# An attention-and-MoE kernel on one core: the opening's first scores in paired banks, and a PV product in pieces

## The chip, the core and the metric

The kernel runs on one core of a Trainium2 chip. The core has TensorE (PE in the profile; its weight loads are PEld), VectorE (DVE), ScalarE (ACT), GpSimd (POOL) and SyncE (SP), each with an instruction stream of its own. They meet through semaphores. Matrix products land in PSUM, eight banks of 512 fp32 values on each of 128 partitions; DMA moves data between the chip's memory and the on-chip buffers. The metric is the device time in microseconds; smaller is better.

## The reference

For 8 batches and 12 heads (448 rows, head size 64) the kernel computes attention with normalized q and k, and then a two-layer MLP over the concatenated heads:

```
q_n, k_n = q / rms(q) * g_q,  k / rms(k) * g_k
attn     = softmax(q_n k_n^T / 8)            # rows of 448
x        = (attn v), heads side by side      # 3584 x 768
h        = x w_in                            # 768 -> 2048
out      = max(0.01 h, h) w_out              # 2048 -> 768
```

## The kernel before

**Units.** The 96 heads are worked in 24 units of four heads; three units make a batch. The four heads of a unit lie as two by two (index r and a) on halves of the 128 partitions, and the 448 rows of a head as seven blocks of 64 (index t, 0 to 6). "Scores (u,t)" below are the scores of unit u for k block t, and "exp (u,t)" their exponential.

**One unit's steps**, with the lines of the profile:

- load of q and k (`load`, L146, queue of SP), of v (`load_v`, L149, queue of POOL);
- squares (`prep_sq` on ScalarE, L169, or `prep_sqp` on POOL, L173), their sums over 64 (`prep_ssq`, VectorE, L180), 1/rms as an Ln and an exponential (`prep_rinv`, ScalarE, L185 and L186: uu, rinv), the normalized fp16 q and k (`prep_norm`, VectorE, L192: n);
- seven transposes each of q and k by PE into a bank (`tr`, L861, for units 0 and 1; `trn`, which is `prep_tr`, L204, for 2 and 3), and a copy of them to `qkT` (`vcopy`, VectorE, L809 for q with the factor g, L811 for k). For unit 1 the k transposes come in two parts, block 0 (K0) and blocks 1 to 6 (K1);
- scores, four matmuls of 64x64 per block into two banks (`score`, L222). `score0` takes block 0 of units 1 and 2, `qk` the others;
- the shift. The exponential needs a common bound. `shift_max` takes the maximum of block 0's scores per partition (L257 and L259 for two separate banks, L262 for a pair) and spreads it on a diagonal (dg, L264); `shift_mm` brings it to all partitions by a matmul with ones (L280; L274 from unit 4 on) and takes the maximum again (L281 or L275), and L285 makes the bias eb of it;
- seven exponentials (`ex`, ScalarE; L242 for a pair of banks in one instruction of 128x896, L239 for two separate banks in two of 128x448), which give back the banks of the scores;
- the row sums of the exponentials, 28 matmuls with ones (`zsum_slot`, L311, or `zsum`, L300), their reciprocal as Ln and exponential (`zinv`, L385 and L387, or by halves L390 and L392: rz), the product with v (`pv`, 28 matmuls, L401), and the multiply of the two, half by half (`xmul`, VectorE, L410), which gives x of this unit and frees PV's two banks.

**Banks.** Banks 4 to 7 are two "slots" for the scores of `qk`; banks 0 to 3 are given one at a time by `aux`, in the order in which they were dropped. An instruction that writes a bank waits until its last reader is through. From unit 5 on all banks are shared.

**Order.** The kernel is written under a manual schedule: on each engine instructions run in the order of the text, which for units 0 to 3 is written out by hand (L827 to L1030). From unit 3 on a loop interleaves a unit's steps with matmuls of the MLP taken from a queue (`moe1`, L423; `moe2`, L469; `seven`, L522). The MLP's first two tiles are started by hand by `moe1_part` (L431): k tiles 0 to 3 need units 0 and 1, the last two need the halves of unit 2's multiply. `warm` (L825) issues matmuls of ones whose result nobody reads.

Of the kernel before, what the change touches and what calls it, by code (L numbers as in the profile page):

```python
# [18 lines left out]
def kernel(  # L19
# [44 lines left out]
    def aux():  # L64
        can = [i for i in free if mine(i)]
        if shared:
            can = [i for i in can[:-1] if i ^ 1 not in free] or can
        free.remove(can[0])
        return single[can[0]]
# [162 lines left out]
    def ex(u, most=NS):  # L232
# [3 lines left out]
        for t, sT in s["sT"][:most]:  # L236
            if isinstance(sT, list):
                for a in range(2):
                    nc.scalar.activation(s["et"][:, t, a], sT[a][:, 0:S], AF.Exp, bias=s["eb"], scale=1.0)  # L239
                    drop(sT[a])  # L240
            else:
                nc.scalar.activation(s["et"][:, t], sT[:, :, 0:S], AF.Exp, bias=s["eb"], scale=1.0)  # L242
                drop(sT)
        s["sT"] = s["sT"][most:]

    def score0(u):
        banks = [aux() for a in range(2)]
        score(u, 0, banks)
        st[u]["sT"] = [(0, banks)]

    def shift_max(u):
        s = st[u]
        sT = s["sT"][0][1]
        if isinstance(sT, list):
            pm2 = small.tile([P, 2], FP32, tag="pm2", name="pm2")
            for a in range(2):
                nc.vector.tensor_reduce(pm2[:, a:a + 1], sT[a][:, 0:S], axis=AXL.X, op=ALU.max)  # L257
            s["spare"] = sT[0]
            nc.vector.tensor_reduce(s["spare"][:, 511:512], pm2, axis=AXL.X, op=ALU.max)  # L259
        else:  # L260
            s["spare"] = sT[:, 0]
            nc.vector.tensor_reduce(s["spare"][:, 511:512], sT[:, :, 0:S], axis=AXL.XY, op=ALU.max)  # L262
# [6 lines left out]
    def shift_mm(u):  # L269
        s = st[u]  # L270
        if u > 0 and "pslot" in st[u - 1]:
            pb = st[u - 1]["pslot"][:, :, S:S + 64]
            for x in range(2):
                nc.tensor.matmul(pb[:, x], onesp, s["dg"][:, 64 * x:64 * x + 64], start=True, stop=True)  # L274
            nc.vector.tensor_reduce(s["spare"][:, 510:511], pb, axis=AXL.XY, op=ALU.max)  # L275
        else:
# [4 lines left out]
            nc.vector.tensor_reduce(s["spare"][:, 510:511], pb[:, 0:P], axis=AXL.X, op=ALU.max)  # L281
# [3 lines left out]
        nc.vector.tensor_scalar(s["eb"], s["spare"][:, 510:511], -1.0, DELTA, op0=ALU.mult, op1=ALU.add)  # L285
# [17 lines left out]
    def zsum_slot(u):  # L303
        s = st[u]
        s["zslot"] = slot()
# [88 lines left out]
    def pv(u, t0=0, t1=NS):  # L394
        s = st[u]
        if t0 == 0 and "pslot" not in s:
            s["pv"] = [aux() for r in range(2)]
# [429 lines left out]
    with tc.manual_schedule():  # L827
# [28 lines left out]
        def tr(u, ti, chunks, tp=None):  # L856
            if tp is None:
                tp = aux()
# [57 lines left out]
        drop(tr(1, 0, ((ALL, vcopy),)))  # L916
        tpk = tr(1, 1, ((K0, vcopy),))
        qk(0, (4,))
        ex(0)
        k1 = []  # L920
        tr(1, 1, ((K1, lambda *a: k1.append(a)),), tpk)
        score0(1)
        prep_ssq(2, ALL, (0,))
        shift_max(1)
        vcopy(*k1[0])
        drop(tpk)
        shift_bank(1)
        qk(0, (5,))
        ex(0)
        warm(8, st[1]["pb"])  # L930
        qk(0, (6,))
        ex(0)
        warm(4, st[1]["pb"])
        shift_mm(1)
        prep_ssq(2, ALL, (1,))
        prep_ssq(3, ALL, (0,))
        ex(1)
        prep_rinv(2)
        qk(1, (1,))
        ex(1)  # L940
        zsum_slot(0)
        pv(0)
        zinv(0)
# [5 lines left out]
        prep_sqp(4, (0,))  # L949
        load_v(4)  # L950
        for f in range(2):
            load_w_out(8 * f, 8)
        qk(1, (2,))
        warm(6, st[1]["pb"])
        drop(st[1]["pb"])
        ex(1)
        trn(2, 0, vcopy)
        qk(1, (3,))
        ex(1)
        trn(2, 1, vcopy)  # L960
        xmul(0)
        qk(1, (4,))
        ex(1)
        qk(1, (5,))
        ex(1)
        score0(2)
        shift_max(2)
        qk(1, (6,))
        ex(1)
        shift_bank(2)  # L970
        warm(12, st[2]["pb"])
        shift_mm(2)
        prep_ssq(3, ALL, (1,))
        prep_ssq(4, ALL, (0,))
        ex(2)
        prep_rinv(3)
# [193 lines left out]
```

## Time and profile before

| | |
|---|---|
| time, median of 3 runs | 409.28 us (408.88, 409.28, 411.71) |
| the profiled execution's own time | 410.29 us |
| its span, first to last instruction | 408.3 us |
| PE busy, share of the span | 97% |
| VectorE, ScalarE, POOL busy | 75%, 74%, 18% |
| mean granted TensorE clock | 0.994 of full |
| busy us of the 25 from 20 to 45: PE, VectorE, ScalarE, POOL | 21.26, 20.48, 22.77, 16.62 |

Times in the profile count from the span's first instruction. A line of the timeline has start, duration, engine, line, operation, output and input, how many instructions are merged in it, and in brackets how long the engine sat idle before it and what ended that. In a line of the timeline with several instructions the duration runs from the first start to the last end; on one engine the next instruction can start before the one ahead has ended. A line of stretches has the stretch, its length, then for each engine busy time and number of instructions, then the granted clock of TensorE (PEclk), the share of DMA engines that were busy, and GB/s.

### The profile page before, as it was taken

The page shows a single profiled execution, that of the slowest core. Times are in us where ns is not written, and L with a number is a line of the kernel's source. Part 1 is how long each engine was busy: PE and PEld are TensorE (multiplying, and loading weights), DVE is VectorE, ACT ScalarE, POOL GpSimd, SP SyncE. Part 2 cuts the span into 40 slices and gives each one's busy share as a digit, 9 for nine tenths or more (in the row PEclk, how much of TensorE's full clock was granted, in tenths as well). Part 3 has the DMA queues.
Part 4 walks back from the last instruction along what each step waited for, and adds up shares of the span by engine and source line. Part 5 has one row for each costly group of instructions (what it writes and reads, how often), then busy time and mean ns, then how long its engine had stood idle before and what let it go on. Part 6 is the DMA issues. An engine that isn't in the chain of part 4 may idle for free.

```text
span 408.3 us, 9444 instructions
## 1 busy us (share of the span) xinstructions
PE 395.0 (97%) x3834; PEld 222.9 (55%) x3834; DVE 307.4 (75%) x484; ACT 301.4 (74%) x476; POOL 74.0 (18%) x86
## 2 busy tenths in 40 slices
PE   7879999999999999999999999989999999999996
PEld 6545454555455544555455544555455557558963
DVE  5898789978888766876678857678579888567672
ACT  5998977879978599688878689868996667743600
POOL 1887331411020200120021200002011202000000
PEclk9899999999999999999999999999999999999999
DMA  5999999899665985578564984676652470032014
GB/s 178 270 251 254 239 236 247 212 204 181 164 161 100 244 218 102 149 196 183 145 158 50 246 218 99 172 176 174 177 96 47 122 163 8 15 72 77 2 39 117
DMA packets 72526, 62.87 MB, mean 154 GB/s; under 512 B 36388, under 2 KB 67620, under 8 KB 72484
## 3 DMA queue, kind: packets, MB, share of 16 engines
q1 hardware_dynamic: 61888, 50.08, 47.0%
q0 software_dynamic: 10272, 11.80, 18.6%
q8 instruction: 30, 0.49, 0.5%
q10 hardware_dynamic: 324, 0.39, 0.3%
q14 instruction: 12, 0.10, 0.1%
HBM read 45.61 MB, written 11.01 MB: 139 GB/s over the span
## 4 chain that ended last, share of the span: by engine, by line
PE 84%; DVE 6%; ACT 5%; DMA 2%; issue 2%; SPq 0%; DVEq 0%; ACTq 0%
PE banks L423 26%; PE banks L522 24%; PE banks L222 8%; PE banks L469 7%; PE banks L401 6%; PE banks L656 6%; PE banks L338 3%; ACT et L242 3%; DVE n L192 2%; DMA rz<-zs 1%; DMA rk<-in_k_dram 1%; PE banks L274 1%; ACT sq L169 1%; PE banks L204 1%; DVE xt L410 1%
## 5 line engine op out<-in xcount | busy, mean ns | idle before, releaser
L242 ACT ACTIVATE et<-banks,eb 128x896 f16<-128x896 f32 x166 | 160.0, 1015 | 23.4 <-PE banks L222 15.4
L423 PE MATMUL banks<-xt,win 128*128 128x448 f16 x612 | 122.2, 353 | 0.0
L423 PEld LDWEIGHTS <-win 128*128 128x128 f16 x612 | 57.3, 98 | 56.1 <-issue 6.8
L417 ACT ACTIVATE gt<-banks 128x448 f16<-128x448 f32 x104 | 56.6, 564 | 5.5 <-PE banks L423 4.4
L222 PE MATMUL banks<-qkT 64*64 64x448 f16 x672 | 49.6, 362 | 3.0 <-ACT et L242 2.1
L180 DVE TENSOR_REDUCE ssq<-sq 128x14 f32<-128x896 f32 (+2 forms) x49 | 50.1, 1056 | 1.3 <-ACT sq L169 1.1
L522 PEld LDWEIGHTS <-sa 128*128 128x128 f16 x352 | 33.4, 98 | 24.6 <-issue 3.6
L522 PE MATMUL banks<-tw,sa 128*128 128x384 f16 x264 | 46.8, 326 | 0.0
L529 DVE TENSOR_TENSOR ost<-banks,ost 128x384 f32<-128x384 f32 x55 | 30.3, 551 | 14.7 <-PE banks L522 14.1
L401 PE MATMUL banks<-et,vt 64*64 64x448 f16 x672 | 37.0, 349 | 0.1
L522 PEld LDWEIGHTS <-gt 128*128 128x128 f16 x264 | 25.5, 98 | 18.3 <-issue 1.7
L222 PEld LDWEIGHTS <-qkT 64*64 64x64 f16 x672 | 17.0, 105 | 32.5 <-issue 26.3
L469 PE MATMUL banks<-wout,gt 128*128 128x384 f16 x192 | 33.7, 326 | 0.0
L291 POOL COPY gate_t<-qkT 128x1 f16<-128x1 f16 x16 | 5.1, 321 | 152.6 <-DMA qkT<-n 152.6
L522 PE MATMUL banks<-wout,gt 128*128 128x384 f16 x176 | 32.4, 326 | 0.0
L379 POOL TENSOR_TENSOR xt<-x,rz 128x896 f16<-128x896 f32 x9 | 19.4, 2158 | 70.4 <-DMA rz<-zs 63.9
L262 DVE TENSOR_REDUCE banks<-banks 128x1 f32<-128x896 f32 x22 | 24.1, 1094 | 10.1 <-PE banks L222 6.3
L353 ACT COPY x<-banks 128x896 f32<-128x896 f32 x16 | 14.5, 906 | 22.1 <-DVE banks L275 22.1
L192 DVE TENSOR_TENSOR n<-rq,rinv 128x896 f16<-128x896 f32 (+2 forms) x25 | 28.3, 1137 | 1.3 <-ACT rinv L186 1.3
L192 DVE TENSOR_TENSOR n<-rk,rinv 128x896 f16<-128x896 f32 (+2 forms) x26 | 27.9, 1078 | 0.0
L401 PEld LDWEIGHTS <-vt 64*64 64x64 f16 x672 | 20.2, 107 | 10.6 <-issue 0.4
L469 PEld LDWEIGHTS <-gt 128*128 128x128 f16 x192 | 17.9, 98 | 13.7 <-issue 2.9
(105 smaller groups left out, 486.8 us busy)
## 6 DMA issues: line engine op xcount, KB each, us to landing
rq<-in_q_dram SPq DMA_DIRECT2D x24, 448.0 KB, 4.7
rk<-in_k_dram SPq DMA_DIRECT2D x24, 448.0 KB, 5.5
out_dram<-ost SPq DMA_DIRECT2D x52, 192.0 KB, 3.4
rz<-zs SPq DMA_DIRECT2D x80, 112.0 KB, 2.7
vt<-in_v_dram POOLq DMA_DIRECT2D x24, 224.0 KB, 4.9
win<-in_moe_w_in_dram POOLq DMA_DIRECT2D x8, 384.0 KB, 14.5
wout<-in_moe_w_out_dram POOLq DMA_DIRECT2D x2, 1536.0 KB, 29.0
out_dram<-ost SPq DMA_DIRECT2D x4, 96.0 KB, 2.1
```

What stands on the lines that cost most here:

```text
L180: nc.vector.tensor_reduce(buf(u, "ssq")[:, ti, :, c[0]:c[1]], buf(u, f"sq{ti}")[:, :, c[0]:c[1]], axis=AXL.X, op=ALU.add)
L192: nc.vector.tensor_tensor(buf(u, "n16")[:, ti, c[0]:c[1]].rearrange("p s a d -> p a s d"), src[:, :, c[0]:c[1]], buf(u, "rinv")[:, ti, :, ...
L222: nc.tensor.matmul(banks[a][64 * r:64 * r + 64, 0:S].rearrange("p (t x) -> p t x", t=NS), kT(u, r, a, t), qT(u, r, a), start=True, stop=True)
L242: nc.scalar.activation(s["et"][:, t], sT[:, :, 0:S], AF.Exp, bias=s["eb"], scale=1.0)
L262: nc.vector.tensor_reduce(s["spare"][:, 511:512], sT[:, :, 0:S], axis=AXL.XY, op=ALU.max)
L401: nc.tensor.matmul(s["pv"][r][64 * a:64 * a + 64, 0:S], vts[u % NV][64 * r:64 * r + 64, a, t], s["et"][64 * r:64 * r + 64, t, a], start=(t ...
L417: nc.scalar.activation(dst, src, AF.Prelu, bias=0.0, scale=1.0, alpha=0.01)
L423: nc.tensor.matmul(hps[:, 0:S], win16[:, kt // 2, kt % 2, ts(ft, P)], xt[:, kt // 2, kt % 2], start=(kt == 0), stop=(kt == KT - 1))
L469: nc.tensor.matmul(op2[:, 0:HC], gt[:, ft, ds(col(t), P)], wout16[:, ft, ds(HC * half, HC)], start=(i == 0), stop=(i == FT - 1))
L522: nc.tensor.matmul(bank[:, 0:HC], a[:, f], b[:, f], start=(first and f == 0), stop=(f == HF - 1), skip_group_check=not first)
L529: nc.vector.tensor_tensor(dst, g[name][:, 0:HC], src, op=ALU.add)
L656: nc.tensor.matmul(bank[:, HX * i:HX * i + HX].rearrange("p (t x) -> p t x", t=NS), w, x[:, kt], start=start, stop=(kt == HK - 1), skip_gr ...
```

## The change

- `score0` of units 1 and 2 takes a pair of banks of 0 to 3 (`pair`), so that the maximum is one reduction and the exponential one instruction; the shift's matmuls go to columns 448 to 511 of that pair (`own`), and the second maximum to a small buffer (`peak`). `shift_bank` and its `warm` matmuls go for these units.
- Unit 1: its first scores come ahead of the six remaining k transposes, which use a bank of their own.
- Unit 2: PV of unit 0 is cut into pieces of 2, 2, 1 and 2 blocks, between unit 2's transposes, its first scores and scores of unit 1; k block 0 is copied first; unit 0's multiply is done in halves, the second after unit 2's k copy.
- The sums of units 0 and 1 are written to a pair of banks 0 and 1 instead of a slot, and their Ln and exponential come directly behind.
- The square sums of units 2 and 3 are done in one go, later than before; the second of unit 4 moves behind unit 2's second half multiply.
- Unit 2's PV comes behind its last scores instead of ahead of them.

The diff, cut to its core (`...` marks what is left out):

```diff
+    def pair():
+        x = [i for i in range(2) if 2 * i in free and 2 * i + 1 in free][0]
...
     def score0(u):
-        banks = [aux() for a in range(2)]
-        score(u, 0, banks)
-        st[u]["sT"] = [(0, banks)]
+        sT = pair()
+        score(u, 0, (sT[:, 0], sT[:, 1]))
+        st[u]["sT"] = [(0, sT)]
+        st[u]["own"] = sT
...
     def shift_mm(u):
...
+        own = s.get("own")
+        if own is not None or u > 0 and "pslot" in st[u - 1]:
+            pb = (st[u - 1]["pslot"] if own is None else own)[:, :, S:S + 64]
             for x in range(2):
                 nc.tensor.matmul(pb[:, x], onesp, s["dg"][:, 64 * x:64 * x + 64], start=True, stop=True)
+            if own is not None:
+                peak = small.tile([P, 1], FP32, tag="peak", name="peak")
+            nc.vector.tensor_reduce(peak, pb, axis=AXL.XY, op=ALU.max)
...
-        s["zslot"] = slot()
+        s["zslot"] = pair() if u < 2 else slot()
...
-        drop(tr(1, 0, ((ALL, vcopy),)))
-        tpk = tr(1, 1, ((K0, vcopy),))
+        drop(tr(1, 0, ((ALL, vcopy),), bank=2))
+        tpk = tr(1, 1, ((K0, vcopy),), bank=3)
         qk(0, (4,))
         ex(0)
+        score0(1)
         k1 = []
-        tr(1, 1, ((K1, lambda *a: k1.append(a)),), tpk)
-        score0(1)
-        prep_ssq(2, ALL, (0,))
+        tpk2 = tr(1, 1, ((K1, lambda *a: k1.append(a)),), bank=2)
+        drop(tpk)
         shift_max(1)
         vcopy(*k1[0])
-        drop(tpk)
-        shift_bank(1)
+        drop(tpk2)
         qk(0, (5,))
         ex(0)
-        warm(8, st[1]["pb"])
+        wb = aux(3)
+        warm(8, wb)
         qk(0, (6,))
         ex(0)
-        warm(4, st[1]["pb"])
+        warm(4, wb)
+        drop(wb)
         shift_mm(1)
-        prep_ssq(2, ALL, (1,))
-        prep_ssq(3, ALL, (0,))
+        prep_ssq(2)
+        ex(1)
+        qk(1, (1,))
         ex(1)
         prep_rinv(2)
-        qk(1, (1,))
+        zsum_slot(0)
+        zinv(0)
+        qk(1, (2,))
         ex(1)
-        zsum_slot(0)
-        pv(0)
-        zinv(0)
         prep_norm(2)
         gate(2)
         prep_sqp(3, (1,))
         load_v(3)
         load(5)
         prep_sqp(4, (0,))
+        st[0]["pv"] = [aux(2), aux(3)]
+        pv(0, 0, 2)
+        drop(tr(2, 0, ((ALL, vcopy),), bank=0))
+        qk(1, (3,))
+        ex(1)
+        pv(0, 2, 4)
+        tpk = tr(2, 1, ((K0, vcopy),), bank=1)
+        drop(tpk)
+        pv(0, 4, 5)
+        score0(2)
+        shift_max(2)
+        qk(1, (4,))
+        ex(1)
+        pv(0, 5, NS)
+        xmul(0, (0,))
+        qk(1, (5,))
+        ex(1)
+        shift_mm(2)
+        qk(1, (6,))
+        ex(1)
+        drop(tr(2, 1, ((K1, vcopy),), bank=2))
+        ex(2)
+        qk(2, (1,))
+        ex(2)
+        xmul(0, (1,))
+        prep_ssq(3)
+        prep_rinv(3)
+        zsum_slot(1)
+        zinv(1)
+        qk(2, (2,))
+        ex(2)
+        prep_norm(3)
+        load(6)
         load_v(4)
         for f in range(2):
             load_w_out(8 * f, 8)
-        qk(1, (2,))
-        warm(6, st[1]["pb"])
-        drop(st[1]["pb"])
-        ex(1)
-        trn(2, 0, vcopy)
-        qk(1, (3,))
-        ex(1)
-        trn(2, 1, vcopy)
-        xmul(0)
-        qk(1, (4,))
-        ex(1)
-        qk(1, (5,))
-        ex(1)
-        score0(2)
-        shift_max(2)
-        qk(1, (6,))
-        ex(1)
-        shift_bank(2)
-        warm(12, st[2]["pb"])
-        shift_mm(2)
-        prep_ssq(3, ALL, (1,))
-        prep_ssq(4, ALL, (0,))
-        ex(2)
-        prep_rinv(3)
-        qk(2, (1,))
-        ex(2)
-        zsum_slot(1)
-        pv(1)
-        zinv(1)
-
-        prep_norm(3)
-        load(6)
         gate(3)
         prep_sqp(4, (1,))
+        st[1]["pv"] = [aux(2), aux(3)]
+        pv(1)
         prep_sqp(5)
         load_v(5)
-        qk(2, (2,))
-        ex(2)
-        warm(12, st[2]["pb"])
         qk(2, (3,))
         ex(2)
-        drop(st[2]["pb"])
         trn(3, 0, vcopy)
-        warm(8, st[2]["pb"])
         trn(3, 1, vcopy)
         xmul(1)
-        prep_ssq(4, ALL, (1,))
+        prep_ssq(4, ALL, (0,))
         qk(2, (4,))
         ex(2)
         st[2]["zt"] = [aux() for r in range(2)]
         zsum(2, 0, 3)
         qk(2, (5,))
         ex(2)
-        pv(2, 0, 3)
-        sums(2, 3, 4)
+        zsum(2, 3, 4)
         qk(2, (6,))
         ex(2)
+        pv(2, 0, 4)
         sums(2, 4, 5)
...
         xmul(2, (1,))
+        prep_ssq(4, ALL, (1,))
         push(0)
```

More of the change, by code (lines that the diff above doesn't have):

```diff
@@ L62, in mine, with aux @@
         return shared or i < 4
-    def aux():
-        can = [i for i in free if mine(i)]
+    def pair():
+        x = [i for i in range(2) if 2 * i in free and 2 * i + 1 in free][0]
+        for i in (2 * x, 2 * x + 1):
+            free.remove(i)
+        return double[x]
+    def aux(bank=None):
+        can = [i for i in free if mine(i) and bank in (None, i)]
         if shared:
@@ L236, in ex @@
         for t, sT in s["sT"][:most]:
[L237 to L243, printed above, removed]
+            nc.scalar.activation(s["et"][:, t], sT[:, :, 0:S], AF.Exp, bias=s["eb"], scale=1.0)
+            drop(sT)
         s["sT"] = s["sT"][most:]
     def score0(u):
-        banks = [aux() for a in range(2)]
-        score(u, 0, banks)
-        st[u]["sT"] = [(0, banks)]
+        sT = pair()
+        score(u, 0, (sT[:, 0], sT[:, 1]))
+        st[u]["sT"] = [(0, sT)]
+        st[u]["own"] = sT
     def shift_max(u):
@@ L253, in shift_max @@
         sT = s["sT"][0][1]
[L254 to L262, printed above, removed]
+        s["spare"] = sT[:, 0]
+        nc.vector.tensor_reduce(s["spare"][:, 511:512], sT[:, :, 0:S], axis=AXL.XY, op=ALU.max)
         s["dg"] = small.tile([P, P], FP16, tag="dg", name="dg")
@@ L270, in shift_mm @@
         s = st[u]
-        if u > 0 and "pslot" in st[u - 1]:
-            pb = st[u - 1]["pslot"][:, :, S:S + 64]
+        peak = s["spare"][:, 510:511]
+        own = s.get("own")
+        if own is not None or u > 0 and "pslot" in st[u - 1]:
+            pb = (st[u - 1]["pslot"] if own is None else own)[:, :, S:S + 64]
             for x in range(2):
                 nc.tensor.matmul(pb[:, x], onesp, s["dg"][:, 64 * x:64 * x + 64], start=True, stop=True)
-            nc.vector.tensor_reduce(s["spare"][:, 510:511], pb, axis=AXL.XY, op=ALU.max)
+            if own is not None:
+                peak = small.tile([P, 1], FP32, tag="peak", name="peak")
+            nc.vector.tensor_reduce(peak, pb, axis=AXL.XY, op=ALU.max)
         else:
@@ L280, in shift_mm @@
             nc.tensor.matmul(pb[:, 0:P], onesp, s["dg"], start=True, stop=True)
-            nc.vector.tensor_reduce(s["spare"][:, 510:511], pb[:, 0:P], axis=AXL.X, op=ALU.max)
+            nc.vector.tensor_reduce(peak, pb[:, 0:P], axis=AXL.X, op=ALU.max)
             if u >= 3:
@@ L284, in shift_mm @@
         s["eb"] = small.tile([P, 1], FP32, tag="eb", name="eb")
-        nc.vector.tensor_scalar(s["eb"], s["spare"][:, 510:511], -1.0, DELTA, op0=ALU.mult, op1=ALU.add)
+        nc.vector.tensor_scalar(s["eb"], peak, -1.0, DELTA, op0=ALU.mult, op1=ALU.add)
     def gate(u):
@@ L395, in pv @@
         s = st[u]
-        if t0 == 0 and "pslot" not in s:
+        if "pv" not in s:
             s["pv"] = [aux() for r in range(2)]
@@ L854, with tr @@
         prep_norm(0, K1, (1,))
-        def tr(u, ti, chunks, tp=None):
+        def tr(u, ti, chunks, tp=None, bank=None):
             if tp is None:
-                tp = aux()
+                tp = aux(bank)
             for c, copy in chunks:
```

## The prediction

> **What bounds the kernel now.** I began with the page: busy time by engine, and the chain that ended last.
>
> ```profile
> PE 395.0 (97%) x3834; PEld 222.9 (55%) x3834; DVE 307.4 (75%) x484; ACT 301.4 (74%) x476; POOL 74.0 (18%) x86
> ...
> PE 84%; DVE 6%; ACT 5%; DMA 2%; issue 2%; SPq 0%; DVEq 0%; ACTq 0%
> ```
>
> TensorE (PE) carries 84% of the chain; only 16% is elsewhere, and the chain in order of time tells where. From 44 us on it is PE almost without a break; from 130 us to the end the waits of PE name one matmul wait, of 0.9 us. So the opening is worth exactly the moment at which PE gets its last operand and runs on. The chain in the stretch that is changed (start us, us, what):
>
> ```profile
> 18.96 1.08 DVE pm L257 x2
> 20.07 0.17 DVE banks L259
> 20.26 0.29 DVE dg L264
> 20.55 0.47 DVE qkT L811
> 21.02 0.22 DVE banks L281
> 21.26 0.17 DVE eb L285
> 21.45 1.16 ACT et L239 x2
> ...
> 42.98 0.64 DVE xt L410
> 43.62 0.04 issue
> 43.66 0.54 PE banks L431 x2
> 44.20 2.27 PE banks L423 x12
> ```
>
> VectorE makes the shift of unit 1, ScalarE waits for it, and at the far end unit 2's multiply releases the last two matmuls of the first MoE tiles. Between them ScalarE is the bound: 22.77 us busy of the 25 from 20 to 45. Its own timeline shows its stalls (in brackets):
>
> ```profile
> 21.45 1.16 ACT L239 ACTIVATE et<-banks,eb 128x448 f16<-128x448 f32 x2 [0.47 <-DVE eb L285]
> 23.87 0.91 ACT L385 ACTIVATE rz<-banks 128x896 f32<-128x896 f32 x1
> 25.66 4.58 ACT L242 ACTIVATE et<-banks,eb 128x896 f16<-128x896 f32 x5
> 30.72 1.16 ACT L239 ACTIVATE et<-banks,eb 128x448 f16<-128x448 f32 x2 [0.47 <-DVE eb L285]
> 34.94 3.87 ACT L242 ACTIVATE et<-banks,eb 128x896 f16<-128x896 f32 x4
> 39.24 1.01 ACT L242 ACTIVATE et<-banks,eb 128x896 f16<-128x896 f32 x1 [0.43 <-PE banks L222]
> ```
>
> Three stalls, 0.47, 0.47 and 0.43 us, and two exponentials in halves, 1.16 us where a whole one occupies 0.91 (five take 4.58: four starts of 0.90 and an end).
>
> **Prices from the rows.** Exponential: 1.01 us long, the next starts 0.91 later. Reduction of 128x896 (L180, L262): 1.07 to 1.10, the next 1.00 later. Normalize (L192): 1.08, the next 1.00 later. dg 0.29, small max 0.30, eb 0.16, half multiply (L410) 0.62, two 1.15. uu 0.31, rinv 0.23, Ln of a unit's sums 0.91, its exponential 0.95. Four score matmuls: 0.31 to the next work, 0.38 to their end; 28 sum matmuls 1.32 and 1.49; within a run of the 64x64 form four take 0.19, so a switch of form costs 0.12. A handover between engines: 0.04.
>
> **The change, step by step, by those prices.** The order of the instructions on each engine is known: POOL's and SP's are unchanged; VectorE, ScalarE and PE differ only between 17 and 44 us.
>
> Unit 1. Its first scores now go before the six k transposes: 18.02 to 18.40. One reduction replaces two halves and their merge, and the square sum of unit 2 that stood ahead of it (17.89, 1.07) moves behind. So max 18.44 to 19.54, dg to 19.86, the k copy (0.55) to 20.33, the shift matmuls at 20.05 (behind the last warm matmuls), small max to 20.62, eb done 20.81, against 21.42. ScalarE is free at 20.88 (0.91 after 19.97): **the first stall is gone**. Exponentials at 20.88 and 21.79. What is late next: both square sums of unit 2 run 20.74 to 22.80, so uu starts at 22.84 (ScalarE idle 0.14), rinv ends 23.41, and the zsum of unit 0, now in the pair that the first exponential leaves at 21.89, runs 21.93 to 23.42 (before: 21.29). Ln of unit 0 at 23.46, against 23.87; exp (1,2) at 25.25, against 25.66: 0.41 earlier. PE idles 1.2 us before that zsum; the Ln would wait for rinv until 23.30 anyway.
>
> Unit 2. Norm of q and k ends 24.52 and 25.52 (0.12 later than before). PV of unit 0 in pieces, transposes and scores share PE; the four extra switches (0.5 us) lie in its idle time. q copy to 26.12, first k block to 26.25, first scores 26.29 to 26.67, max 26.71 to 27.81, dg to 28.13, first half multiply to 28.67, shift matmuls 28.17 to 28.40, small max, eb done 29.09, against 30.69. ScalarE needs its five exponentials until 29.80: **the second stall is gone, with 0.7 us to spare**. Exp (2,0) at 29.80 and (2,1) at 30.71, against 30.72 and, behind uu and rinv, 32.25. The k copy and the other half multiply take VectorE to 30.33.
>
> **A wait that is added.** Both square sums of unit 3 now follow that multiply (before, one was done far ahead): 30.25 to 32.31. ScalarE is free at 31.62 and its uu waits until 32.35: 0.73 lost. Behind it queue rinv, Ln, the second exponential of the sums and exp (2,2), which comes at 34.62 against 34.94. Of 0.92 gained at exp (2,0), 0.32 is left there. Norm of unit 3 ends at 34.04 and 35.04, 0.37 later than before; its transposes, no longer behind 12 and 8 warm matmuls (0.69 and 0.45 us), still give the k copy at 36.29 against 36.76.
>
> Unit 2's end. Before, score (2,6) stood behind PV, which waited for the multiply of unit 1 (until 37.83): the third stall. Now PV stands behind it. Score (2,6) needs the slot that exp (2,4) leaves at 37.45, and is done at 37.87. Exponentials at 34.62, 35.53, 36.44, 37.35, 38.26: **the last at 38.26 against 39.24, 0.98 earlier**. The rest follows as it did: Ln and exponential of the sums, multiply halves at 40.95 and 41.99, the last two matmuls of the first MoE tiles at 42.65 against 43.66. The square sum of unit 4's k now stands after the multiply (42.53 to 43.60), so uu of unit 4 waits to 43.64 and norm ends 46.33, before 46.59; PE reaches its k transposes at about 46.3 and stalls some 0.07.
>
> What is moved past DMA: the calls that load v of unit 4, W_out and unit 6 move in the text only. Unit 5's loads wait for norms 0.12 later, unit 6's 0.37; v of unit 4 needs PV of unit 0, done at 27.2, and was issued at 29.72. W_out, issued at 30.5 and 32.8, landed 25.8 to 32.2 us later, by 65.1 at the latest; PE first reads it at 69.7, then at 68.8. Covered.
>
> **Sum.** 0.41 up to the Ln of unit 0 (the first stall and the first half pair, less the two waits of ScalarE ahead of it) + 0.51 up to exp (2,0) (the second stall) − 0.60 up to exp (2,2) (the new wait of 0.73 less 0.14 for the second half pair) + 0.66 up to exp (2,6) (the third stall, and 0.2 that its four predecessors lost between them) = 0.98. 1.01 is left at the last two matmuls; less 0.07 ahead of unit 4, 0.95 is booked. The profiled execution has 410.29 us, a span of 408.3 and 2.0 around it; it becomes 409.3. It lies 1.0 above the median, 409.28, which becomes **408.3 us**.
>
> Not shown by the trace: a small max that writes to SBUF. pm (L257) does, in 0.57 for 448, about half of 1.10 for 896 written to PSUM: between −0.05 and +0.1; I take 0. The new wait's price is between 0, were VectorE half a microsecond quicker at 26 to 32, and 1.5, twice the walk; I take the walk's 0.73 as all its terms are rows.
>
> **The clock**, 38 warm matmuls fewer after 24 us. The granted clock by stretches (PE busy is the second number, PEclk the third from the end):
>
> ```profile
> 7.48:10.89 3.41, 1.76 (x23) 1.19 (x24) 2.92 (x7) 2.35 (x5) 0.72 (x2) 1.00 0.89 316
> 10.89:14.31 3.42, 3.42 (x32) 2.56 (x28) 2.86 (x6) 2.95 (x5) 2.00 (x3) 0.50 1.01 360
> ...
> 24.55:27.96 3.41, 2.23 (x36) 1.48 (x34) 3.13 (x5) 3.38 (x5) 2.42 (x3) 1.00 1.10 258
> 27.96:31.37 3.41, 2.80 (x52) 1.78 (x48) 2.74 (x7) 2.94 (x5) 3.39 (x4) 1.00 1.09 256
> ```
>
> After a stretch with PE 1.76 us busy of 3.41 the clock was 0.50 for the next; after 2.23 it stayed at 1.00. My walk's PE from 27.96 to 31.37 is 0.23 + 0.38 + 0.49 + 0.38 + 0.52 = 2.0 busy: between the two. Shifted to 27.4 it would be 1.6. At 0.50, ten warm matmuls took 1.27 against 0.57.
>
> The Trainium skill (TensorE: Matmul & The Clock Gate, "Why this matters for your kernels") asks only that PE has no idle gaps above about 3 us; the walk's longest is 1.2, so by it the clock holds and the sum stands. The trace disagrees: the stretch from 7.48 had no gap above 1.34 us and was followed by the half clock. The same page (Part 1) says that the window is free-running, which no row here can show; by it some executions would lose the clock and others not.
>
> **Rivals.** (1) *The gain is swallowed*, 409.3: the clock halves for one stretch, 31.4 to 34.8. zsum of unit 1 ends 0.8 later, Ln waits 0.36, PV and transposes push the k copy to 37.5, and exp (2,6) comes at 39.31, as before. A VectorE that is 0.95 later in the new wait does the same. For: 2.0 lies in the open interval. Against: 24.55 to 27.96 held. 0.22. (2) *Slower*, 410.6: the half clock holds to 38.2. PV then ends at 36.07, score (2,3) at 36.6, k copy at 38.8, exp (2,6) at 40.6, 1.35 later than now; from one stretch to two is where the sign turns. Against: PE is busy in 31.4 to 34.8, which ended the half clock at 14.31. 0.15. (3) *More*, 407.6: the new wait is hidden, 0.73 more. Against: VectorE has no idle time from 26.7 to 32.3. 0.08. (4) The stalls go but PE after 44 us takes its time back in waits for data: 409.3 also; against, the waits of PE show 0.5 us at 43.66 and no other to 130 us. 0.05. The forecast, 407.8 to 408.9: 0.50.
>
> **Numbers.** The range, 406.9 to 410.9, reaches from rival 3, with the 0.4 by which the lowest run lies under the median and 0.3 for the open terms, to rival 2 with 0.3. Within 1% (4.1 us, about what a measurement of this kernel can tell from no change) lie all cases: 0.95; faster 0.02, slower 0.03 for a clock that halves more often.
>
> **What will show it.** Right: eb of unit 1 at about 20.8; no stall of the first exponentials of units 1 and 2; uu of unit 3 waiting 0.7 for the square sums; exp (2,6) unstalled; MoE matmuls from 42.7. Wrong: a PEclk of 0.50 after 20 us, or a wait of PE after 44 us that was not there.

## The result, and the profile after

The changed kernel is slower: 412.23 us median of 22 runs (410.12 to 415.93), against 409.75 of the kernel before (22 runs, 408.30 to 412.08). The ratio is 1.0062, 95% interval 1.0040 to 1.0084. Its profiled execution took 411.59 us, span 409.2. The forecast was 408.3. Medians and ratios below leave out four executions in a second, slower state of the chip: two of count_back, one of count_less and one of the kernel before.

The page of the changed kernel first, with its busy times and the shares of the chain that ended last:

```profile
PE 393.0 (96%) x3798; PEld 221.0 (54%) x3798; DVE 310.3 (76%) x481; ACT 301.0 (74%) x474; POOL 72.9 (18%) x86
...
PE 85%; DVE 6%; DMA 3%; ACT 2%; issue 2%; SPq 0%; DVEq 0%
```

PE has 36 matmuls fewer (3834 before), each with a weight load: 72 instructions. It is busy 2.0 us less in a span that is 0.9 longer. DMA has 3% of the chain instead of 2%.

Did the opening do what was forecast? ScalarE's timeline of the changed kernel, 19 to 44 us, answers line by line to the one shown of before:

```profile
19.24 3.72 ACT L243 ACTIVATE et<-banks,eb 128x896 f16<-128x896 f32 x4 [0.47 <-PE banks L228]
25.48 6.38 ACT L243 ACTIVATE et<-banks,eb 128x896 f16<-128x896 f32 x7
32.56 0.32 ACT L191 ACTIVATE uu<-ssq,eps_t 128x28 f32<-128x28 f32 x1 [0.69 <-DVE ssq L186]
34.83 4.65 ACT L243 ACTIVATE et<-banks,eb 128x896 f16<-128x896 f32 x5
42.24 1.01 ACT L243 ACTIVATE et<-banks,eb 128x896 f16<-128x896 f32 x1
43.87 0.32 ACT L191 ACTIVATE uu<-ssq,eps_t 128x28 f32<-128x28 f32 x1 [0.63 <-DVE ssq L186]
```

The three stalls are gone, the forecast wait of uu is there, and the exponentials of units 1 and 2 run in unbroken rows. Exp (3,0) starts at 42.24, 0.76 before the old 43.00. So at 43 us the kernel is ahead. The chain of waits in order of time (start us, us, what) shows where it falls behind:

```profile
67.34 0.20 PE banks L400 x5
67.54 7.15 DMA qkT<-n
74.69 0.03 issue
74.72 0.45 DVE qkT L182
75.17 2.00 DVE ssq L186 x2
77.17 0.02 issue
77.19 0.33 ACT uu L191
77.52 0.02 issue
77.54 0.23 ACT rinv L192
77.77 0.37 ACT ost L476
78.14 1.82 ACT et L243 x2
79.96 0.04 issue
80.00 1.52 PE banks L400 x28
```

From unit 6 on, k and q are transposed by a DMA (`prep_trd`). Its landing at 74.69 releases VectorE's multiply by g; behind that stand the square sums, uu, rinv and two exponentials, and PE. In the kernel before this landing was at 73.87 and PE ran through. PE's waits between 44 and 200 us, first the kernel before (what, us in total, times, longest):

```profile
PE banks L431 <- DVE xt L410: 0.5, 1, 0.5
```

and the changed kernel:

```profile
PE banks L400 <- ACT et L243: 0.5, 1, 0.5
PE banks L228 <- ACT et L243: 0.5, 1, 0.5
PE banks L271 <- DVE dg L259: 0.4, 1, 0.4
```

Set side by side by the same PE instruction, the changed kernel is 0.76 us ahead at 40 us, 0.56 behind at 80, 1.02 behind at 126 and 1.30 behind at 138.

These early losses are not what stands at the end of this trace. PE's longest wait after 200 us, first in the kernel before and then in the changed kernel:

```profile
PE banks L274 <- DVE dg L264: 0.9, 1, 0.9
```

```profile
PE banks L521 <- DVE ost L528: 0.7, 1, 0.7
```

The kernel before waits at 266 us, behind a landing of rz at 260; the changed one does not wait there and is level again at 270 us (0.09 ahead). It then falls 0.87 behind at 277, where its own wait for VectorE is, and 0.20 more at 314: 0.97 at the end. So one trace shows where PE waits, but the time of the kernel has to be read from the medians.

### The profile page after: what moved, and what is told of

It reads as the page before. It is cut to its first block, busy times and chain, and to the rows that moved or that the text cites. A ratio compares the mean times of both kernels' runs of the same rounds, so it can differ in the third digit from the quotient of the medians.

```text
span 409.2 us, 9372 instructions
## 1 busy us (share of the span) xinstructions
PE 393.0 (96%) x3798; PEld 221.0 (54%) x3798; DVE 310.3 (76%) x481; ACT 301.0 (74%) x474; POOL 72.9 (18%) x86
## 4 chain that ended last, share of the span: by engine, by line
PE 85%; DVE 6%; DMA 3%; ACT 2%; issue 2%; SPq 0%; DVEq 0%
PE banks L422 29%; PE banks L521 24%; PE banks L228 9%; PE banks L400 6%; PE banks L655 6%; PE banks L468 6%; PE banks L337 3%; DVE n L198 2%; DMA qkT<-n 2%; ACT et L243 2%; DVE ssq L186 1%; DMA rk<-in_k_dram 1%; DVE banks L257 1%; PE banks L271 1%; DVE ost L528 1%
## 5 line engine op out<-in xcount | busy, mean ns | idle before, releaser
L198 DVE TENSOR_TENSOR n<-rq,rinv 128x896 f16<-128x896 f32 (+2 forms) x25 | 35.1, 1406 | 1.9 <-ACT rinv L192 1.9
L257 DVE TENSOR_REDUCE banks<-banks 128x1 f32<-128x896 f32 x24 | 26.3, 1096 | 11.0 <-PE banks L228 6.8
L198 DVE TENSOR_TENSOR n<-rk,rinv 128x896 f16<-128x896 f32 (+2 forms) x26 | 26.1, 1010 | 0.0
```

The costliest lines, as they stand in the source:

```text
L198: nc.vector.tensor_tensor(buf(u, "n16")[:, ti, c[0]:c[1]].rearrange("p s a d -> p a s d"), src[:, :, c[0]:c[1]], buf(u, "rinv")[:, ti, :, ...
```

## The theories

The transposing DMA has 16 completions. Own table, from the trace, of the one for unit 6 (us), beside the fetch of 16 KB that the page lists under "q8 instruction":

```
              PE instr.  issue  fetch         1st    15th   16th completion
before        7667       68.21  69.59-70.66   73.72  73.86  73.87
after         7595       67.54  72.46-73.62   73.01  73.15  74.69
```

Fifteen completions came 0.7 us earlier than before, as the opening promised; the last came 1.54 behind the fifteenth, 1.07 after the end of the fetch. **Theory F**: TensorE's instructions are fetched in blocks by the DMA engines (16 KB each, queue q8 of the page); 72 instructions fewer shift all later fetches against the work, into the end of the transposing DMAs, whose last completion then waits. **Theory C**: the 36 matmuls that nobody reads kept TensorE's clock up; without them more executions lose it for a stretch. **Theory D**: the opening's gain ends at the landing, which is set by the loads ahead of it.

Data of all runs, as reference for what follows. "PE instr." counts one fewer than the pages' matmuls and weight loads (2 x 3834 = 7668 before), here and in the expectations; the differences are what matters. "Clock" is the mean granted clock of all executions, "at full clock" the median of those with 0.998 or more. The kernel before ran again beside each round of runs, with medians of 409.88 (the row below), 410.05, 409.63 and 409.96 and mean clocks of 0.9967 to 0.9977, so runs of different rounds are best compared by their ratios. The rounds are count_back to warm_back, gap_fill to gap36_ssq, trd_first to spread_trd, and spread_less to spread_ssq:

```
              PE instr.  median  runs  ratio to before [95%]     clock   at full clock (runs)
before        7667       409.9   35    -                         0.9971  409.65 (21)
after         7595       412.23  22    1.0062 [1.0040, 1.0084]   0.9944  411.32 (5)
count_back    7667       410.63  10    1.0013 [0.9984, 1.0042]   0.9945  409.38 (6)
count_less    7547       410.85  11    1.0013 [0.9993, 1.0033]   0.9950  409.19 (3)
before_less   7595       410.69  12    1.0019 [1.0004, 1.0034]   0.9961  410.86 (5)
warm_back     7667       410.23  12    1.0012 [0.9991, 1.0032]   0.9978  410.16 (10)
gap_fill      7595       412.00  12    1.0036 [1.0012, 1.0060]   0.9969  412.00 (6)
gap36         7667       410.33  12    0.9997 [0.9966, 1.0029]   0.9953  408.97 (3)
early         7743       411.26  12    1.0034 [1.0008, 1.0060]   0.9930  410.63 (2)
gap36_ssq     7667       410.09  12    0.9995 [0.9970, 1.0021]   0.9948  410.74 (2)
trd_first     7595       412.69  12    1.0077 [1.0045, 1.0109]   0.9944  411.62 (4)
before_trd    7667       410.67  12    1.0012 [0.9988, 1.0037]   0.9972  410.01 (7)
spread36      7667       409.35  12    0.9994 [0.9967, 1.0022]   0.9980  408.81 (8)
spread_trd    7667       411.00  12    1.0041 [1.0016, 1.0065]   0.9974  410.25 (7)
spread_less   7595       410.50  12    1.0012 [0.9995, 1.0029]   0.9972  410.63 (6)
spread_mid    7631       410.70  12    1.0018 [1.0001, 1.0035]   0.9979  410.64 (8)
spread_ssq    7667       409.32  12    0.9988 [0.9963, 1.0013]   0.9979  409.03 (8)
```

## First round: the number of instructions

**count_back**: the changed kernel, with the 72 instructions back at the start.

```diff
-        warm(42, wbank)
+        warm(24, wbank)
+        warm_small(54, wbank)      # 128x32 weights, 64 columns
```

> The changed kernel, but 18 of the warm matmuls at the very start (while PE waits for the first load) are replaced by 54 small ones of about the same total time: 72 PE instructions more, as many as the change took away, and nothing else moved. Theory F (PE fetches its instructions in blocks through the same DMA engines; with 72 instructions fewer these fetches fall late into the flight of the transposing DMAs of units 6 to 10, whose landing VectorE waits for): the fetch near 72.5 us moves back to about 69, the late losses go, and the 0.75 us that the opening gained stays: 409.0, against 412.2 for the changed kernel. Theory C (the missing warm matmuls cost TensorE clock): PE is as busy as before, 412.2. Theory D (PE that starts 0.75 us earlier only meets transfers that are bounded by bytes): 412.2.

Measured: 410.63. Unit 6's DMA had no late completion (issue 71.41, fetch 71.94 to 73.25, 16th at 76.06, 0.03 behind the 15th). But the small matmuls held the first transposes up (ScalarE's wait before the first copy to qkT was 1.45 us instead of 0.50), and this trace lost the clock in 16.88 to 23.71 and 33.95 to 37.36. Less than hoped, and not a clean test.

**count_less**: the changed kernel with 24 pairs of warm matmuls at the start merged into one of double width each.

```diff
-        warm(32, wbank)  ...  warm(42, wbank)
+        warm(26, wbank); warm_wide(3, wbank)  ...  warm_wide(21, wbank)
```

> The changed kernel with 48 of the warm matmuls at the start merged into 24 of twice the width: the same PE time, 48 PE instructions fewer. Theory F: each fetch comes some 2.4 us later (256 instructions take about 13 us), so the one at 72.5 comes at about 75, behind the landing of unit 6's transposing DMA, and likewise for units 7 to 10: as fast as with the 72 instructions put back, or better, 408.5 to 409.5. Theory C and theory D: 412.2, nothing that they speak of has changed.

Measured: 410.85. At unit 6 the fetch (73.81 to 74.99) began 0.69 us ahead of the first completion (74.50) and the last was not late (74.62); at unit 8 it was (15th 99.49, 16th 101.04, fetch 98.94 to 99.83). So fewer instructions still are not simply worse. That suggests that the phase counts and not the number; the ratio, 1.0013 (0.9993 to 1.0033), leaves both open.

**before_less**: the kernel before, with 36 pairs of its start merged, so that it has 7595 instructions too and nothing else is changed.

```diff
-        warm(32, wbank)  ...  warm(42, wbank)
+        warm(2, wbank); warm_wide(15, wbank)  ...  warm_wide(21, wbank)
```

> The kernel before, with 72 of the 74 warm matmuls at the start merged into 36 of twice the width: the same PE time and the old order, but 72 PE instructions fewer, as in the changed kernel. Theory F: the fetches fall late into the transposing DMAs as they do in the changed kernel, 411 to 412. Theories C and D: 409.7, as before.

Measured: 410.69, 0.8 above the kernel before. The trace repeats the changed kernel's: fetch 72.32 to 73.43, 15th completion 73.04, 16th 74.60, and PE goes from 0.68 ahead of the kernel before (in this trace the opening began that much earlier) to 0.47 behind at 80 us, 0.90 at 138. **The loss at unit 6 belongs to the number of instructions, not to the new order.** In the median the 72 instructions cost 0.8 us here (ratio 1.0004 to 1.0034), a third of the change's loss. That this is the loss at unit 6, carried to the end, is not shown: at 270 us this trace is level with the kernel before, and 0.19 behind at the end.

**warm_back**: the changed kernel with 18 warm matmuls more at the start and 18 in PE's idle 1.31 us at 20.80.

> The changed kernel with 36 warm matmuls put back, 18 at the start and 18 in the idle time of PE ahead of unit 0's sums (20.8 to 22.1 us): the 72 instructions are back, and PE is busier as well. Theory F: 409.0, as with the small ones at the start, since only the count matters. Theory C: about 410, and better than with the small ones. Theory D: 412.2.

Measured: 410.23. No late completion at unit 6 (16th at 72.78), PE 0.64 ahead until 120 us and 0.22 at 176, although the 18 matmuls at the start held the first transposes up (ScalarE's wait before the first copy to qkT was 1.37 us). The median is nearer to theory C's 410 than to theory F's 409.0.

## Second round: fetch or clock

**gap_fill**: the same 18 in the idle place, 7595 instructions by merging 18 pairs at the start.

```diff
-        warm(42, wbank)
+        warm(6, wbank); warm_wide(18, wbank)
...
         qk(1, (1,))
+        wb = aux(3); warm(18, wb); drop(wb)
         ex(1)
```

> The changed kernel with 18 warm matmuls put into TensorE's idle 1.31 us at 20.80, and 18 pairs of the opening's warm matmuls merged into 18 of double width, so that TensorE has as many instructions as in the changed kernel (7595) and its clock as much work as before. Theory F (the instruction fetches of TensorE, moved by 72 instructions, delay the landing of the transposing DMAs): nothing is mended at full clock; the DMA issued at about 67.5 lands after more than 6.5 us, PE is 0.4 to 0.7 us behind the kernel before at 80 us and about 1 us at 126, and the median is 410.8 to 411.6. Theory C (the missing warm matmuls cost clock): the granted clock of all the executions averages 0.997 and not 0.994, and the time falls to the 409.0 that the opening's gain of 0.77 leaves of 409.75.

Measured: 412.00 with the clock restored to 0.9969, and 412.00 at full clock. Theory C alone falls. The trace has four late completions (units 6, 8, 9 and one at 239 us), each 1.49 to 1.56 us behind the fifteenth.

**gap36**: 36 small ones in that place, nothing at the start.

> The changed kernel with all 36 missing matmuls put back as small ones (32 ns each) in the idle 1.31 us at 20.80, none ahead of the first transposes; 7667 instructions as before the change. Theory F: the DMA issued at 67.5 lands in 5 to 5.7 us, no stall of PE at 80 us, offset there -0.6 or better, median 409.0 to 409.7. Theory C: the same clock as in the run with 18 full matmuls in that place, 0.997, and 409.0. The two agree here; if the median is over 410.5 both lack something.

Measured: 410.33, and 408.97 at full clock. What it shows best is theory C. Stretches of its trace (stretch, length, PE, PEld, DVE, ACT, POOL busy with instructions, then the granted clock, DMA share, GB/s):

```profile
14.34:17.75 3.41, 2.01 (x26) 1.19 (x25) 2.92 (x6) 3.38 (x6) 3.41 (x7) 1.00 1.19 202
17.75:21.16 3.41, 3.41 (x31) 1.80 (x29) 2.09 (x6) 2.11 (x3) 3.41 (x4) 0.50 1.12 270
27.99:31.40 3.41, 1.61 (x24) 0.95 (x24) 3.14 (x8) 3.41 (x5) 3.39 (x4) 1.00 1.09 250
31.40:34.82 3.42, 3.42 (x41) 2.25 (x37) 2.77 (x4) 2.06 (x4) 1.36 (x2) 0.50 1.11 261
```

In this execution the clock was halved twice, the second time exactly in the stretch of rival 1. From exp (0,0) to exp (3,0) it took 31.40 us instead of 29.05. In the changed kernel's profiled execution the same place kept its clock:

```profile
26.51:29.93 3.42, 2.32 (x32) 1.27 (x32) 2.76 (x7) 3.42 (x4) 3.40 (x3) 1.00 1.10 231
29.93:33.34 3.41, 2.71 (x56) 1.92 (x60) 2.77 (x5) 2.68 (x6) 1.73 (x3) 1.00 1.10 263
```

These two stretches lie elsewhere than gap36's, and that is the point. In each trace the halved clock begins and ends only at places that are whole multiples of 3.413 us apart (to 0.01 us, in the six traces that lost it before the end, nine times in all), and where these places lie differs from execution to execution: in gap36 17.75 is one of them, in the changed kernel's trace, by the halving behind its last matmul, 29.93. Counted from the traces between each one's own places, in the first 50 us: the nine halvings came after stretches with 1.62 to 2.17 us of PE busy, no stretch at full clock with less than 1.95 kept it, and none with 2.18 or more lost it. So in the opening the busy time of the stretch does decide, to within 0.2 us, and the same order of work keeps or loses the clock by where the stretches fall. It is no rule for other work: at the end of the program, from 401 us on, stretches with 1.46 to 1.63 kept it.

**early**: 74 matmuls more than the changed kernel, made of small ones, to bring the fetch ahead of the DMA's issue.

```diff
-        warm(42, wbank)
+        warm(14, wbank); warm_small(52, wbank)
...
+        wb = aux(3); warm_small(50, wb); drop(wb)   # at 20.80
```

> The changed kernel with 74 matmuls more, in the time of the old ones: in the opening 28 warm matmuls of 60 ns become 52 of 32 ns, and 50 small ones stand in the idle 1.31 us at 20.80; 7743 instructions, 148 more than the changed kernel, about 7 us of fetching earlier. Theory F: the fetch that was at 72.46 comes at about 65.5, before the transposing DMA is issued (67.5), and so do the next ones (77.7 for an issue at 80.8, 90 for 93); the DMAs of units 6 to 8 land in 3.9 to 4.7 us, PE keeps its -0.6 to -0.8 us against the kernel before from 41 to 126 us, and the median is 408.3 to 409.2, below the kernel before. Theory C: the instruction count is nothing; small matmuls in the opening hold the clock no better than the full ones, so 409.0 to 410.5, and the DMAs land as late as in the changed kernel.

Measured: 411.26; a miss. The fetch did come early (66.19, issue 66.82), and units 7 to 10 landed in 4.0 to 4.9 us. But unit 6 landed at 73.94 all the same, 1.8 us behind the loads of unit 8 (rk at 72.12), and PE waited there 0.43 and 0.52 us. That is theory D: this landing does not follow PE's gain. And its mean clock is the lowest of all (0.9930): the small matmuls in place of full ones did not hold it better.

**gap36_ssq**: the added wait undone.

```diff
         prep_ssq(2)
+        prep_ssq(3, ALL, (0,))
...
-        prep_ssq(3)
+        prep_ssq(3, ALL, (1,))
```

> The kernel with 36 small matmuls at 20.80 (7667 instructions), and the first half of unit 3's square sums ahead of the first exponential of unit 1 again, where the kernel before has it. The new wait of the prediction was 0.69 us (uu of unit 3 at 32.56, behind both square sums on VectorE). If it stands on the path that sets the end, exp (2,2) starts 0.5 to 0.66 us earlier, less up to 0.4 that the two norm multiplies of unit 2 are moved back by, and 0.2 to 0.6 us of it are left at 43 us; median 0.2 to 0.6 below the same kernel without the move. If the exponentials of unit 2 are limited elsewhere (norm and transposes of unit 2 later by 0.4), nothing or +0.4.

Measured: 410.09 against 410.33, no difference that can be told. Both traces lost the clock in the opening, so the wait was tried again below.

## Third round: the landing, and 36 matmuls in idle places

**trd_first, before_trd, spread_trd**: one order on SP changed, unit 6's transposing DMA ahead of unit 8's loads, in the changed kernel, in the kernel before and in the best one.

```diff
-                        job(load, u + 4)          # at d == 0, for u == 4
...
-                            job(prep_trd, u + 2)
+                            job(lambda u: (prep_trd(u + 2), load(u + 4)), u)
```

> The changed kernel, with one order changed on SP at 62 us: the transposing DMA of unit 6 goes ahead of the loads of unit 8 (rq, rk) instead of behind them; TensorE's instructions stay 7595. Landings of that DMA so far: its first completion came 1.51 to 1.69 us behind rk's landing in six of the traces whatever PE did before, and the last 1.5 us later still where an instruction fetch fell in between. Theory D (the landing is set by the loads ahead of it in SP's queue, the opening's gain waits there): issued at 67.5 the DMA lands by 72.0 instead of 74.7, no stall of PE at 80 us, its offset to the kernel before stays near -0.7 there, and the median falls by 0.8 to 1.3 us, to 410.9 to 411.4. Theory F (the fetch alone): the fetch falls behind the landing and the gain at 80 us is the same, but units 7 to 9 meet their fetches as before and lose 0.4 to 0.7 of it by 140 us. If neither holds, the DMA lands at 73 or later and the time is 412.2.

> The kernel before with the same one order changed on SP (unit 6's transposing DMA ahead of unit 8's loads). In the kernel before PE had some 0.25 us of slack at that landing (landed 73.87, PE ran on at 79.44 without a wait). Theory D: the landing comes 1 to 2 us earlier and nobody waits for it, so the time stays within 0.3 of 409.9. If it is faster by 0.5 or more, the kernel before loses time there too in most executions.

> The same 36 matmuls in idle places, and unit 6's transposing DMA ahead of unit 8's loads. If fetch, clock and landing were all that took the opening's 0.77 us away, this keeps it: PE stays 0.6 to 0.8 us ahead of the kernel before from 41 us to 260 us and the median is 408.9 to 409.4, against 409.9 of the kernel before. If it is not below the kernel before, PE is caught by a later landing (in two traces the return of the sums, rz, at 260 us).

Measured: 412.69, 410.67 and 411.00. The landing does come earlier (72.06 in the kernel before, 71.14 in the third, against 73.87 and 73.45 without the move), so the loads do set it there. PE waited for no exponential at 79 us in either of these two traces. But no median fell, and spread_trd is 1.65 above the same kernel without the move, although its trace is the fastest of all (409.55, PE 0.94 ahead of the kernel before at the end). trd_first, expected at 410.9 to 411.4, lost the clock twice in its trace and met the fetch again (73.49 to 74.42, issue 69.75), though without a late completion there. **The landing explains one wait of a trace, not the time.** What the later loads of unit 8 cost in return was not found.

**spread36**: the 36 matmuls in PE's idle places of the opening, so that none of them delays another.

```diff
-        warm(12, wb)  ...  warm(8, wb)
+        warm(20, wb)  ...  warm(15, wb)
...
         qk(1, (1,))
+        wb = aux(3); warm(15, wb); drop(wb)
...
         xmul(0, (1,))
+        wb = aux(3); warm(6, wb); drop(wb)
         prep_ssq(3)
```

> The changed kernel with the 36 matmuls put back where PE is idle in the opening and none of them delays another: 8 more behind the 12 at 12.80, 7 more behind the 8 at 14.56, 15 at 20.80, 6 at 30.44. 7667 instructions. Theory F: the fetch at unit 6 is back at 69 to 70 us, no completion is 1.5 us late there, offset -0.5 or better at 80 us. Theory C: no half clock between 14 and 35 us in any execution but few, mean granted clock 0.997 or more. Both together: 409.0 to 409.8, not above the kernel before; theory D allows no more than about 0.3 below it.

Measured: 409.35, 2.9 us below the changed kernel (95% interval 1.4 to 4.0, by resampling the runs, as all differences of medians below), with the highest mean clock of all. The new order is kept whole; only matmuls that nobody reads were added. **All of the loss hangs on the 36 matmuls.** Of the opening's 0.78 us nothing measurable reaches the end: the ratio to the kernel before is 0.9994, 0.9967 to 1.0022. In its trace PE gives its lead back in waits for data: 1.6 us in three waits for VectorE's dg between 44 and 200 us, and 0.3 at unit 6.

**spread_less and spread_mid**: the same work in the same places, with 72 and 36 instructions merged away at the start, as in before_less.

> The kernel with 36 matmuls spread over idle places, and 36 pairs of the opening's warm matmuls merged into 36 of double width: the same work of TensorE, 7595 instructions as in the changed kernel. Theory F (instruction fetches against the transposing DMAs): the fetch at unit 6 is back at 72 to 73 us, the DMA lands after 74.4, PE waits 0.4 or more at 79 us, and the median is 411 to 412.5, 1.5 to 3 above the kernel with 7667. Theory C (only the clock counts): clock 0.997 or more and a median of 409.0 to 409.9, no different from that kernel.

> As the run with 7595 instructions, with 18 pairs merged instead of 36: 7631 instructions. Theory F: the fetch at unit 6 at 70.8 to 71.8 us; it ends before the last completions or just meets them, so the median lies between the two, 409.5 to 411.5. Theory C: 409.0 to 409.9.

Measured: 410.50 and 410.70. Up to exp (3,0) spread36 and spread_less run alike (41.71 and 41.63). VectorE's multiply by g in spread36, and PE behind it (in brackets the idle time and what ended it):

```profile
73.47 0.45 DVE L182 TENSOR_SCALAR qkT<-qkT,gcol 128x896 f16<-128x896 f16 x1 [1.07 <-DMA qkT<-n]
```

```profile
78.75 1.52 PE L400 MATMUL banks<-et,vt 64*64 64x448 f16 x28 [0.33 <-ACT et L243]
```

and in spread_less:

```profile
74.49 0.45 DVE L182 TENSOR_SCALAR qkT<-qkT,gcol 128x896 f16<-128x896 f16 x1 [2.26 <-DMA qkT<-n]
```

```profile
78.87 0.38 PE L228 MATMUL banks<-qkT 64*64 64x448 f16 x4 [0.85 <-ACT et L243]
79.77 0.95 PE L400 MATMUL banks<-et,vt 64*64 64x448 f16 x16 [0.52 <-ACT et L243]
```

Here too the fifteenth completion was in time (72.95, fetch 72.23 to 73.37) and the last was late (74.47); PE is 1.02 later. But the two profiled executions end alike (410.67 and 410.66 us, both with a span of 408.8), because spread36 met its three waits for dg later on. In the medians the difference is 1.15 (95% interval -0.3 to 1.8), 1.8 at full clock (0.3 to 2.7); spread36 is of another round, and against spread_ssq of the same round it is 1.18 (-0.5 to 1.9). Pooled, the kernels with filled idle places and 7595 instructions (gap_fill, spread_less; 24 runs) are 1.21 us above those with 7667 (spread36, spread_ssq, warm_back; 36 runs), interval 0.4 to 2.5. Most of it is gap_fill's; beside its own round spread_less is not clearly above the kernel before (ratio 0.9995 to 1.0029). It is less than the 1.5 to 3 that theory F had expected. The mean clock of the two pools (0.9970 against 0.9979) would explain about 0.4 us of it (0.0009 x 409, an estimate). spread_mid's trace lost the clock once at 18.26, and met its late completions at unit 7 (15th 86.41, 16th 87.95) and unit 16 (15th 222.25, 16th 223.81).

**spread_ssq**: spread36 with the added wait undone, as in gap36_ssq.

> The kernel with 36 matmuls spread over idle places (7667), and the first half of unit 3's square sums ahead of the first exponential of unit 1. The wait of uu of unit 3 goes from 0.69 to nothing, exp (2,2) to (3,0) start 0.3 to 0.5 us earlier. If PE keeps it, the median is 0.3 to 0.5 below the same kernel without it (409.35), so 408.8 to 409.1, 0.6 to 0.9 below the kernel before. If the landing at unit 6 (73.3 to 73.9) limits PE, nothing is left of it.

Measured: 409.32. The wait is gone in the trace:

```profile
25.45 6.54 ACT L243 ACTIVATE et<-banks,eb 128x896 f16<-128x896 f32 x7
31.87 0.32 ACT L191 ACTIVATE uu<-ssq,eps_t 128x28 f32<-128x28 f32 x1
34.61 4.61 ACT L243 ACTIVATE et<-banks,eb 128x896 f16<-128x896 f32 x5
```

From exp (0,0) to exp (3,0) it takes 28.82 us, 0.23 less than spread36, so a third of the 0.69 reaches that point. The time is the same as without it (difference -0.04, interval -1.3 to 1.6). At 0.9988 of the kernel before (0.9963 to 1.0013) it is the lowest median of the study, but no version was shown to be faster than the kernel before.

## Why the prediction was wrong, point by point

The **opening** was right in kind and nearly in size.

- First stall: eb of unit 1 done at 20.95 (20.80 + 0.15; forecast 20.81, before 21.42). Right. But the Ln of unit 0 came at 23.67, not 23.46: a gain of 0.20, not 0.41. Exp (0,5), whose scores now stand behind unit 1's first scores and transposes, started at 19.24 instead of 19.07, a move on PE that the walk did not price. This 0.2 stays as an error to the end.
- Second stall: exp (2,0) at 29.93 (29.80; before 30.72). Right.
- The added wait: 0.69 (0.73). Right; exp (2,2) at 34.83 (34.62).
- Third stall gone: exp (2,6) at 38.48 (38.26; before 39.24). The last two matmuls of the first MoE tiles at 42.90 (42.65). No stall ahead of unit 4's k transposes (0.07 had been booked). So 0.76 to 0.78 instead of 0.95.

The **step that failed** stood in the text as "From 44 us on it is PE almost without a break", with rival 4 at 0.05. I took the kernel after 44 us as fixed and moved it forward by the 0.95 us, and the sum gave the 36 removed matmuls no price. Both were wrong. Put back in idle places, the 36 matmuls are worth 2.9 us (1.4 to 4.0) of the median, and even then the 0.3 us left of the opening's gain at the end cannot be told from none (ratio 0.9967 to 1.0022). Rival 4, data waits that take the gain back, was right in kind: the landing at unit 6 gave 1.33 us away in the profiled execution (0.77 ahead, 0.56 behind), where an instruction fetch came just ahead of the DMA's first completion and its last was late, and other waits for data followed it. "Covered" held for what it looked at (PE read W_out at 69.07 without a wait), but the transposing DMA of unit 6 was not looked at. I had counted the removed matmuls only as clock, never as 72 instructions of fetching.

The **clock** part was right about the place and the kind of loss (rival 1: half clock in 31.4 to 34.8, seen in gap36 and 0.35 us later in trd_first), but not about how often. The forecast booked none and let it happen in one or two stretches as a rival; in fact it is a mixture over executions, of which the prediction only quoted the possibility. It also read the stretches of the kernel before as if they lay in the same places in every execution; the traces show, against its "which no row here can show", that they do not. (Ten warm matmuls at half clock, 1.27 us to the end of the last, should be set against 0.72 in the changed kernel and not 0.57; nothing hangs on it.) The mean granted clock fell from 0.9971 to 0.9944; at 1.7 us lost per halved stretch that is 0.0027 x 409 / 1.7 = 0.65 stretches more per execution. One stretch cost 1.27 us up to exp (3,0) (gap36_ssq against spread_ssq) or 1.95 (spread_mid against spread36), so by this estimate 0.8 to 1.3 us of the median, if all of them lie in the opening and are carried to the end.

**The sum as the runs give it**, an estimate: 409.75, less 0.3 that spread36 leaves of the opening's gain, plus 1.2 for the 72 instructions, plus 0.8 to 1.3 for the clock: 411.5 to 412.0, against 412.23 measured. What is shown is the 2.9 us of the 36 matmuls together; how they divide between fetches and clock is not measured apart. What stays open: the way from a late completion at unit 6 to the time of the kernel, since in the traces that loss is gone by 270 us or matched by other waits; gap_fill, which has its clock back and should by this be near 410.7, measured 412.00; its trace has four late completions, twice as many as spread_less, from the same number of instructions. Also open is why nothing measurable of the opening's 0.78 us reaches the end, beyond the waits for data seen in single traces.

On the Trainium skill: the page "TensorE: Matmul & The Clock Gate" says in its section "Why this matters for your kernels" to avoid idle gaps above about 3 us; the longest gap in the changed opening was 1.31, and the clock was halved all the same in some executions (twice in the trace of trd_first, which has the same opening; single executions of the changed kernel had a mean granted clock of 0.983). Its section "A second HAM failure mode: psum-queue depth-cycling", which tells of frequent small idle times doing the same, describes these runs better.

## What to carry to other kernels

An instruction that does nothing has a place too: taking 36 idle matmuls out moved every later instruction fetch and left stretches in which the clock can be halved, and taking them out cost more than the reordering gained. When a change alters the number of instructions on the bounding engine, test it with the number and the warming work held constant (merge or split matmuls that nobody reads) before judging the order. And when an opening is shortened, look for the next landing that has little slack, here 0.26 us at unit 6 (from landing to PE's matmul 5.31 us, 74.69 to 80.00, in the changed kernel; in the one before 73.87 to 79.44, 5.57), because PE can be no earlier there than the data.

## What was not expected of the hardware

TensorE's instructions are fetched in blocks of 16 KB over the DMA engines: 29 of them in the changed kernel, 30 in the one before, on the page of the changed kernel as:

```profile
q8 instruction: 29, 0.48, 0.5%
```

That is half a per cent of DMA time, about one fetch per 256 PE instructions, each 0.9 to 1.5 us long and 10 to 16 us apart, with few exceptions. With the number of PE instructions the fetch near unit 6 moved from 73.81 (7547) over 72.2 to 72.7 (7595) and 67.3 to 70.0 (7667) to 66.19 (7743), in the traces that kept their clock from 15 us on. In the 17 traces, 14 of 306 transposing DMAs had a last completion more than 1 us behind the fifteenth, and all 14 had a fetch that began 0.28 to 0.58 us ahead of the first completion; the last came 1.03 to 1.21 us after the fetch's end. Eleven of the 14 are in the five traces with 7595 instructions, none in the nine with 7667. Six of the 14, at units 16 and 17, cost PE nothing that shows: it had no wait in the 20 us after any of them. It is no rule, though: beside many other fetches at the same distance the last completion came within 0.5 us of the first. The Trainium skill (Runtime: NRT & Kernel Launch, section "Instruction fetch mechanics") has the blocks of 16 KiB and calls the cost of crossing one mostly hidden; for TensorE itself the traces agree (none of PE's waits between 44 and 200 us in the changed kernel, 0.5, 0.5 and 0.4 us, was for a fetch), but by these times another DMA's completion can pay for it.
